# States in one software-queue load, a split first x load, and scores at other slots in an attention + GELU kernel

## Chip, cores, metric

One NeuronCore of a Trainium2 chip. The metric is the device time of one execution in microseconds (us), the median over several runs. The kernel before takes 268.34 us (three runs, 267.02 to 268.4). A profiled run adds a trace; its span, from first to last instruction, is some 2 us shorter than the device time. In the traces PE is TensorE (matmuls), PEld its weight loads, ACT is ScalarE (exp, GELU, copies), DVE is VectorE (copies, sums), POOL is GpSimd and SP is SyncE. A load issued by gpsimd goes through the software queue, one issued by SP or ACT through a hardware queue.

## The reference, cut to what matters

```python
# x: 8 batches x 8 heads x 512 x 64,  state: 8 x 8 x 32 x 64
scores = scale * x @ state.T            # softmax over 32 states   -> a
xread  = a @ state
scores2 = scale * state @ x.T           # softmax over 512 rows    -> a2
sread  = a2 @ x
h = concat([xread, sread], axis=2)      # -> 4352 rows x 512
out = gelu(h @ w_in) @ w_out            # w_in 512 x 2048, w_out 2048 x 512
```

The kernel folds `state @ w_in` into a matrix P per batch, so that `gelu(a @ P) @ w_out` gives the rows of xread.

## The kernel before

Names used below: `M` is one pair of matmuls into an `hp` PSUM buffer plus a GELU on ACT; `U` is four matmuls into an `op` buffer and, in its last quarter, a copy on DVE and a store from SP; `pmat` makes P. PSUM buffers are those that matmuls write; x^T is x transposed, A^T the transposed attention weights of xread. Batches 1 to 7 run in a loop of eight slot pairs `p`, two `M` each. Scores, `hp` and `p_ps` all share four PSUM buffers (`ps_f`).

The states of batches 1 to 7 come as fourteen loads from SP, after the first normalisation of batch 0. On the memory side the slowest dimension is `c`, four heads:

```python
st_rows = state.rearrange("b (c t) n d -> b t c n d", t=2)
...
def load_states():
    for b in range(1, B):
        for t in range(2):
            nc.sync.dma_start(out=st_f[:, b, t, :], in_=st_rows[b, t])
```

x of batch 0 comes in two software-queue (gpsimd) loads that cast to bf16. The order in the loop:

```python
for b in range(1, B):
    nb = b + 1
    for p in range(2 if b == 1 else 0, 8):
        k = 16 * b + 2 * p
        if p == 2 and nb < B:
            scores(nb, 0); scores(nb, 1); norm(nb, 0); norm(nb, 1)
        ...                       # p == 5: A^T of nb and x^T of nb + 1 by DMA transpose on SP
        M(k, k + 1)
        ...                       # last batch: also the rows of sread
        while u < k - 4:
            U(u); u += 1
        if p == (2 if b == 1 else 1):
            pmat(b, (2, 3), act=(1,))
            ...                   # and two U more, which leaves pair 2 without a U
```

The softmax here doesn't subtract the row's maximum and nothing guards it: scores larger than these inputs give would overflow.

Of the kernel before, what the change touches and what calls it, by code (L numbers as in the profile page):

```python
# [9 lines left out]
FP32 = mybir.dt.float32  # L10
BF16 = mybir.dt.bfloat16
# [6 lines left out]
def kernel(  # L18
# [8 lines left out]
    nc = tc.nc  # L27

    B, H, S, D = x.shape
    _, _, NS, _ = state.shape  # L30
# [3 lines left out]
    HC = H // 2  # L34
    MC = d_ff // 128
    SJ = S // 128
    FC = d_ff // 512

    persist = ctx.enter_context(tc.tile_pool(name="persist", bufs=1))
# [5 lines left out]
    ps_f = ctx.enter_context(tc.tile_pool(name="ps_f", bufs=4, space=PSUM))  # L45
# [8 lines left out]
    ident = persist.tile([128, 128], BF16, name="ident")  # L54
    sbd = persist.tile([128, B, HC, 2 * NS], BF16, name="sbd")
    XSR = persist.tile([128, HC, B * NS], BF16, name="XSR")
    g_sr = persist.tile([128, MC, B * NS], BF16, name="g_sr")
    st_f = persist.tile([128, B, 2, D], FP32, name="st_f")
    st_bf = persist.tile([128, B, 2, D], BF16, name="st_bf")
    gate = persist.tile([128, HC], FP32, name="gate")  # L60
    ones = persist.tile([128, HC], BF16, name="ones")
    warm = persist.tile([128, 512], BF16, name="warm")
    x4s = [persist.tile([128, SJ, HC, 128], BF16, name=f"x4_{i}") for i in range(2)]


    st_rows = state.rearrange("b (c t) n d -> b t c n d", t=2)
    for t in range(2):
        eng = nc.scalar if t == 0 else nc.sync
        eng.dma_start(out=st_f[:, 0, t, :], in_=st_rows[0, t])
    nc.vector.memset(warm, 0.0)  # L70
    nc.vector.memset(ones, 1.0)
    xbs = {0: xin.tile([128, H, SJ * D], BF16, name="xb", tag="xb")}
    xr = x.rearrange("b h (p j) d -> b p h (j d)", j=SJ)
    for i in range(2):
        hs = slice(4 * i, 4 * i + 4)
        nc.gpsimd.dma_start(out=xbs[0][:, hs, :], in_=xr[0, :, hs, :])
    make_identity(nc, ident)
    nc.vector.memset(sbd, 0.0)

    def load_w_in(f):  # L80
        nc.gpsimd.dma_start(
            out=w_in_bf[:, :, f * 512:(f + 1) * 512],
            in_=moe_w_in[:, f * 512:(f + 1) * 512].rearrange("(c p) f -> p c f", c=HC),
        )
# [6 lines left out]
    def load_x(b):  # L91
        xb = xin.tile([128, H, SJ * D], BF16, name="xb", tag="xb")
        nc.gpsimd.dma_start(out=xb, in_=xr[b])
        xbs[b] = xb
# [1 line left out]
    load_w_in(0)  # L96
    load_w_out(0)
    load_w_in(1)

    def load_states():  # L100
        for b in range(1, B):
            for t in range(2):
                nc.sync.dma_start(out=st_f[:, b, t, :], in_=st_rows[b, t])  # L103

    def load_rest():
        load_x(1)
# [8 lines left out]
    def keep_warm(n):  # L115
        ps = ps_o.tile([128, 512], FP32, name="warm_ps", tag="op")
        for _ in range(n):
            nc.tensor.matmul(ps, lhsT=warm[:, 0:128], rhs=warm, start=True, stop=True)


    def state_prep(b0, b1):
        n = b1 - b0
        nc.vector.tensor_copy(out=st_bf[:, b0:b1, :, :], in_=st_f[:, b0:b1, :, :])  # L123
        ps = ps_f.tile([128, n, HC, NS], BF16, name="st_ps", tag="f")
        for b in range(b0, b1):
            nc.tensor.transpose(  # L126
                ps[:, b - b0, :, :].rearrange("p c n -> p (c n)"),
                st_bf[:, b, :, :].rearrange("q t d -> q (t d)"),
                ident,
            )  # L130
        for t in range(2):
            src = ps[64 * t:64 * t + 64, :, :, :].rearrange("d b c n -> d (b c) n")
            dst = sbd[64 * t:64 * t + 64, b0:b1, :, 32 * t:32 * t + 32].rearrange(
                "d b c n -> d (b c) n"
            )
            nc.vector.tensor_copy(out=dst, in_=src)


    class Att:
# [2 lines left out]
    atts = {}  # L142

    def begin(b):
        A = Att()
        atts[b] = A
        A.x4 = x4s[b % 2]
        A.xT = att.tile([128, SJ, HC, 128], BF16, name="xT", tag="xT")
        A.e = att.tile([128, SJ * 2, HC * NS], BF16, name="e", tag="e")
        A.a = att.tile([128, SJ * 2, HC * NS], BF16, name="a", tag="a")  # L150

    def rearr(b):
        A = atts[b]
        eng = nc.vector if b < 2 else nc.gpsimd
        for t in range(2):
            eng.tensor_copy(  # L156
                out=A.x4[:, :, :, 64 * t:64 * t + 64].rearrange("p j c d -> p c j d"),
                in_=xbs[b].rearrange("p (c t) (j d) -> p t c j d", t=2, d=D)[:, t],
            )


    def xtr(b, cs):
        A = atts[b]
        xv = xbs[b].rearrange("p (c t) (j d) -> p j c t d", t=2, d=D)
        ps = ps_f.tile([128, len(cs), SJ, 128], BF16, name="xT_ps", tag="f")
        for i, c in enumerate(cs):
            for j in range(SJ):
                for t in range(2):
                    nc.tensor.transpose(ps[64 * t:64 * t + 64, i, j, :], xv[:, j, c, t, :], ident)  # L169
        out = A.xT[:, :, cs[0]:cs[0] + len(cs), :].rearrange("p j c n -> p c j n")  # L170
        if b == 0 and cs[0] == 0:
            nc.scalar.copy(out=out, in_=ps)
        else:
            nc.vector.tensor_copy(out=out, in_=ps)

    def xtr_dma(b):
        A = atts[b]
        nc.sync.dma_start_transpose(
            out=A.xT.rearrange("p j c n -> p (j c) n"),
            in_=A.x4.rearrange("p j c n -> p (j c n)"),  # L180
        )
# [68 lines left out]
    def atr(b):  # L250
        A = atts[b]
        A.AT = att.tile([128, SJ, 2, 128], BF16, name="AT", tag="AT")
        if b == 0:
            for t in range(2):
                ps = ps_f.tile([128, SJ, 128], BF16, name="aT_ps", tag="f")
                for j in range(SJ):
                    nc.tensor.transpose(ps[:, j, :], A.a[:, 2 * j + t, :], ident)
                o, i = A.AT[:, :, t, :], ps
                if t == 0:
                    nc.vector.tensor_copy(out=o, in_=i)  # L260
                else:
                    nc.scalar.copy(out=o, in_=i)
            return
        ps = ps_f.tile([128, 2, SJ, 128], BF16, name="aT_ps", tag="f")
        for t in range(2):
            for j in range(SJ):
                nc.tensor.transpose(ps[:, t, j, :], A.a[:, 2 * j + t, :], ident)
        nc.vector.tensor_copy(out=A.AT.rearrange("p j t n -> p t j n"), in_=ps)

    def atr_dma(b):  # L270
        A = atts[b]
        A.AT = att.tile([128, SJ, 2, 128], BF16, name="AT", tag="AT")
        nc.sync.dma_start_transpose(
            out=A.AT.rearrange("p j t n -> p (j t) n"), in_=A.a
        )
# [140 lines left out]
    def M(*ms):  # L416
        for m in ms:
            mm1(m // MC, m % MC)

    def U(*us):  # L420
        for u in us:
            mm2(u // 16, u % 16 // 4, u % 4)

    begin(0)
    keep_warm(6)
    state_prep(0, 1)
    xtr(0, (0, 1))
    scores0(0)
    scores0(1)
    xtr(0, (2, 3))  # L430
    norm0(0)
    nc.vector.memset(st_f[0:1, 1, 0, 0:1], 0.0)
    load_states()
    norm0(1)
    scores0(2)
    norm0(2)
# [5 lines left out]
    nc.scalar.activation(out=gate, in_=ones, func=AF.Gelu)  # L442
    keep_warm(3)
    atr(0)
    rearr(0)


    M(0, 1, 2, 3)
# [2 lines left out]
    U(2)  # L451
    M(4)
    U(3)
    state_prep(1, B)
    begin(1)
    xtr(1, (0, 1))
    xtr(1, (2, 3))
    M(5)
# [38 lines left out]
    u = 16  # L497
    for b in range(1, B):
        nb = b + 1
        for p in range(2 if b == 1 else 0, 8):  # L500
            k = 16 * b + 2 * p
            if p == 2 and nb < B:
                scores(nb, 0)
                scores(nb, 1)
                norm(nb, 0)
                norm(nb, 1)
            if p == 5 and nb < B:
                atr_dma(nb)
                if nb + 1 < B:
                    begin(nb + 1)  # L510
                    rearr(nb + 1)
                    xtr_dma(nb + 1)
                    if nb + 3 < B:
                        load_x(nb + 3)
            M(k, k + 1)
            if nb == B:
                mm1_sr(2 * p)
                mm1_sr(2 * p + 1)
            while u < k - 4:
                U(u)  # L520
                u += 1
            if p == (2 if b == 1 else 1):
                pmat(b, (2, 3), act=(1,))
            if p == 6 and nb < B:
                pmat(nb, (0, 1), act=(1,))
            if p == (2 if b == 1 else 1) or p == 6 and nb < B:
                if u >= 16:
                    U(u, u + 1)
                    u += 2
            if p == 4 and nb < B:  # L530
                sread(nb)
            if p == 6 and nb < B:
                srt(nb)
    while u < 16 * B - 4:
        U(u)
# [34 lines left out]
```

## Time and profile before

| | before |
|---|---|
| device time, median | 268.34 us |
| profiled span | 266.8 us |
| TensorE busy | 220.7 us (83%) |
| ACT, DVE busy | 121.3 us, 81.5 us |
| TensorE waits named by the trace | 24.3 (states), 5.7 (x^T of batch 2), 2.7 (exp), 2.4 (first x) us |

In the slices one digit is the busy share, in tenths, of one fortieth of the span; PEclk is the clock that the throttle granted to TensorE, in the same tenths. The wait view lists for each pair of instruction groups the total idle time, how often, and the longest. The lines themselves stand in the prediction.

### The profile page before, as it was taken

What the parts mean: (1) busy time and instruction counts of PE and PEld (TensorE: products, weight loads), DVE (VectorE), ACT (ScalarE), POOL (GpSimd) and SP (SyncE); (2) the same over time, 40 slices, a digit from 0 to 9 for tenths busy, and PEclk for the clock granted to TensorE, in tenths of its full rate; (3) what the DMA queues carried; (4) which work ended last, traced back from release to release, by engine and by line L of the source; (5) the groups of instructions that cost most, each with busy time, mean ns of one, the idle gap of its engine ahead of it and who ended that gap; (6) DMA issues with size and microseconds to landing.
All of it is one profiled execution on the core that took longest, in us unless ns stands there. A gap on an engine that the chain in (4) does not pass through costs nothing.

```text
span 266.8 us, 4389 instructions
## 1 busy us (share of the span) xinstructions
PE 220.7 (83%) x1867; PEld 101.8 (38%) x1867; DVE 81.5 (31%) x160; ACT 121.3 (45%) x214; POOL 28.7 (11%) x38
## 2 busy tenths in 40 slices
PE   4794000998918999999999989998998999999992
PEld 1431000643302444444444434444443445455540
DVE  2421000564516021912552172246025520500032
ACT  1371000282608344945574475449445745544200
POOL 6290000242000030040012003000000000000000
PEclk9999555699985899999999999999999999999999
DMA  7999992066260860466253047012903200400015
GB/s 89 192 172 186 202 144 40 2 79 80 79 157 1 120 79 3 157 123 76 81 133 66 0 157 109 11 77 83 122 0 143 56 4 0 158 2 0 0 41 195
DMA packets 38643, 22.82 MB, mean 86 GB/s; under 512 B 21856, under 2 KB 34400, under 8 KB 38624
## 3 DMA queue, kind: packets, MB, share of 16 engines
q0 software_dynamic: 12560, 8.39, 22.3%
q1 hardware_dynamic: 25788, 14.00, 21.2%
q8 instruction: 14, 0.23, 0.3%
q10 hardware_dynamic: 276, 0.16, 0.2%
q14 instruction: 5, 0.04, 0.0%
HBM read 17.30 MB, written 8.91 MB: 98 GB/s over the span
## 4 chain that ended last, share of the span: by engine, by line
PE 70%; SPq 9%; DMA 8%; ACT 5%; DVE 4%; issue 2%; DVEq 0%; ACTq 0%; POOLq 0%
PE op L376 38%; PE hp L346 18%; SPq L103 9%; DMA st_f<-in_state_dram 4%; PE p_ps L322 3%; PE hps L390 3%; PE ops L402 3%; DMA xb<-in_x_dram 2%; ACT L227 2%; DMA xT<-x 2%; PE sr L286 2%; PE xT_ps L169 1%; ACT e L227 1%; ACT g L353 1%; DVE a L243 1%
## 5 line engine op out<-in xcount | busy, mean ns | idle before, releaser
L376 PE MATMUL op<-w_out_bf,g 128*128 128x512 bf16 x512 | 123.8, 383 | 0.3
L353 ACT ACTIVATE g<-hp 128x512 bf16<-128x512 f32 x128 | 67.9, 601 | 84.5 <-PE hp L346 84.4
L376 PEld LDWEIGHTS <-g 128*128 128x128 bf16 x512 | 48.8, 98 | 63.2 <-issue 8.0
L346 PE MATMUL hp<-AT,P 128*128 128x512 bf16 x256 | 66.7, 388 | 3.1 <-ACT e L227 2.7
L346 PEld LDWEIGHTS <-P 128*128 128x128 bf16 x256 | 23.8, 99 | 31.0 <-issue 7.0
L336 DVE CAST P<-p_ps 128x512 bf16<-128x512 f32 x32 | 20.7, 684 | 39.2 <-PE p_ps L322 39.1
L366 DVE COPY osb<-op 128x512 f32<-128x512 f32 x31 | 20.8, 687 | 36.6 <-PE op L376 36.6
L334 ACT CAST P<-p_ps 128x512 bf16<-128x512 f32 x32 | 17.5, 588 | 24.0 <-PE p_ps L322 14.9
L156 POOL COPY x<-xb 128x1024 bf16<-128x1024 bf16 x12 | 12.6, 1083 | 129.7 <-PE sr L286 129.7
L126 PE MATMUL st_ps<-ident,st_bf 128*128 128x128 bf16 x8 | 1.2, 308 | 24.3 <-DVE st_bf L123 24.3
L227 ACT ACT_TABLE_LOAD x7 | 9.0, 1283 | 10.3 <-PE pt L220 6.7
L322 PE MATMUL p_ps<-w_in_bf,sbd 64*32 64x512 bf16 x256 | 12.4, 403 | 1.3 <-ACT g L353 1.3
L240 DVE TENSOR_REDUCE cs<-e 128x16 f32<-128x512 bf16 x14 | 9.5, 681 | 12.9 <-ACT e L227 12.9
L243 DVE TENSOR_TENSOR a<-e,ics 128x512 bf16<-128x512 bf16 x14 | 10.5, 750 | 0.6
L126 PEld LDWEIGHTS <-st_bf 128*128 128x128 bf16 x8 | 0.8, 136 | 25.6 <-DVE st_bf L123 25.6
L220 PE MATMUL pt<-sbd,xT 128*128 128x64 bf16 x112 | 4.8, 200 | 5.7 <-DMA xT<-x 5.7
L366 DVE COPY osb<-ops 128x512 f32<-128x512 f32 x2 | 1.4, 692 | 26.3 <-PE ops L402 26.3
L353 ACT ACT_TABLE_LOAD x7 | 9.0, 1283 | 0.1
L123 DVE CAST st_bf<-st_f 128x128 bf16<-128x128 f32 (+1 forms) x2 | 0.9, 426 | 26.5 <-DMA st_f<-in_state_dram 26.5
L390 PE MATMUL hps<-XSR,w_in_bf 128*128 128x256 bf16 x64 | 8.3, 273 | 0.0
L295 DVE RECIPROCAL inv<-sr 128x2 f32<-128x2 f32 x8 | 1.4, 169 | 21.9 <-PE sr L286 21.9
L227 ACT ACTIVATE e<-pt 128x512 bf16<-128x512 f32 x14 | 7.6, 594 | 0.1
(55 smaller groups left out, 104.6 us busy)
## 6 DMA issues: line engine op xcount, KB each, us to landing
out_dram<-osb SPq DMA_DIRECT2D x31, 256.0 KB
xb<-in_x_dram POOLq DMA_DIRECT2D x7, 512.0 KB, 6.8
w_in_bf<-in_moe_w_in_dram POOLq DMA_DIRECT2D x4, 512.0 KB, 11.6
w_out_bf<-in_moe_w_out_dram POOLq DMA_DIRECT2D x4, 512.0 KB, 12.2
xb<-in_x_dram POOLq DMA_DIRECT2D x2, 256.0 KB, 5.4
out_dram<-osb SPq DMA_DIRECT2D x8, 64.0 KB
st_f<-in_state_dram SPq DMA_DIRECT2D x15, 32.0 KB
out_dram<-osb SPq DMA_DIRECT2D x1, 128.0 KB
```

What stands on the lines that cost most here:

```text
L103: nc.sync.dma_start(out=st_f[:, b, t, :], in_=st_rows[b, t])
L156: eng.tensor_copy(out=A.x4[:, :, :, 64 * t:64 * t + 64].rearrange("p j c d -> p c j d"), in_=xbs[b].rearrange("p (c t) (j d) -> p t c j d" ...
L227: nc.scalar.activation(out=A.e[:, :, 64 * half:64 * half + 64], in_=pt.rearrange("p j t c n -> p (j t) (c n)"), func=AF.Exp, scale=scale,)
L243: nc.vector.tensor_tensor(out=A.a[:, :, hs].rearrange("p g (c n) -> p g c n", n=NS), in0=e4, in1=ics[:, :, :].to_broadcast((128, G, 2, NS) ...
L322: nc.tensor.matmul(ps[t][32 * c:32 * c + 32, :], lhsT=sbd[64 * t:64 * t + 64, b, c, 32 * t:32 * t + 32], rhs=w_in_bf[64 * t:64 * t + 64, c ...
L334: nc.scalar.copy(out=dst, in_=ps[t])
L336: nc.vector.tensor_copy(out=dst, in_=ps[t])
L346: nc.tensor.matmul(hp, lhsT=Ps[b][:, t, m * 128:(m + 1) * 128], rhs=atts[b].AT[:, :, t, :], start=(t == 0), stop=(t == 1),)
L353: nc.scalar.activation(out=gs[b][:, m, :], in_=hp, func=AF.Gelu)
L366: nc.vector.tensor_copy(out=osb, in_=ps)
L376: nc.tensor.matmul(ps, lhsT=gs[b][:, m, j * 128:(j + 1) * 128], rhs=w_out_bf[:, m, :], start=(m == 0), stop=(m == MC - 1),)
L390: nc.tensor.matmul(hp, lhsT=w_in_bf[:, c, m * 128:(m + 1) * 128], rhs=XSR[:, c, :], start=(c == 0), stop=(c == HC - 1),)
```

## The change

It means to take away each of the four waits: states as one bf16 load on the software queue, early; x of batch 0 half over the hardware queue as fp32 and half over the software queue, so that both halves come sooner, with x^T copied in quarters; and the next batch's scores at another slot pair. Core of the diff:

```diff
-    st_rows = state.rearrange("b (c t) n d -> b t c n d", t=2)
+    st_rows = state.rearrange("b (e h) n d -> (h n) b e d", e=2)
+    nc.scalar.dma_start(out=st_f, in_=st_rows[:, 0, :, :])
+    for c in range(2):
+        nc.sync.dma_start(out=x0f[:, 2 * c:2 * c + 2, :], in_=xr[0, :, 2 * c:2 * c + 2, :])
...
+    nc.gpsimd.dma_start(out=xbs[0][:, 4:8, :], in_=xr[0, :, 4:8, :])
...
     load_w_in(1)
-    def load_states(): ...            # fourteen nc.sync.dma_start
+    nc.gpsimd.dma_start(
+        out=st_bf[:, 1:B, :, :].rearrange("q b e d -> q (b e) d"),
+        in_=st_rows[:, 1:B, :, :].rearrange("q b e d -> q (b e) d"),
+    )
...                                    # state_prep: four half transposes a batch; x^T in quarters;
...                                    # A^T in two halves, both copied on DVE
-            if p == 2 and nb < B:
+            if p == (4 if b == 1 else 1) and nb < B:
                 scores(nb, 0)
...
-            if p == 5 and nb < B:
+            if p == (7 if b == 1 else 4) and nb < B:
                 atr_dma(nb)
-                if nb + 1 < B:
+            if p == (7 if b == 1 else 5) and nb + 1 < B:
...
-            if p == (2 if b == 1 else 1):
+            if p == 3:
                 pmat(b, (2, 3), act=(1,))
...
-            if p == 4 and nb < B:
+            if p == 5 and nb < B:
                 sread(nb)
```

More of the change, by code (lines that the diff above doesn't have):

```diff
@@ L57 @@
     g_sr = persist.tile([128, MC, B * NS], BF16, name="g_sr")
-    st_f = persist.tile([128, B, 2, D], FP32, name="st_f")
+    st_f = persist.tile([128, 2, D], FP32, name="st_f")
     st_bf = persist.tile([128, B, 2, D], BF16, name="st_bf")
+    x0f = persist.tile([128, HC, SJ * D], FP32, name="x0f")
     gate = persist.tile([128, HC], FP32, name="gate")
@@ L63 @@
     x4s = [persist.tile([128, SJ, HC, 128], BF16, name=f"x4_{i}") for i in range(2)]
-    st_rows = state.rearrange("b (c t) n d -> b t c n d", t=2)
-    for t in range(2):
-        eng = nc.scalar if t == 0 else nc.sync
-        eng.dma_start(out=st_f[:, 0, t, :], in_=st_rows[0, t])
+    xr = x.rearrange("b h (p j) d -> b p h (j d)", j=SJ)
+    st_rows = state.rearrange("b (e h) n d -> (h n) b e d", e=2)
+    nc.scalar.dma_start(out=st_f, in_=st_rows[:, 0, :, :])
+    for c in range(2):
+        nc.sync.dma_start(out=x0f[:, 2 * c:2 * c + 2, :], in_=xr[0, :, 2 * c:2 * c + 2, :])
     nc.vector.memset(warm, 0.0)
@@ L72 @@
     xbs = {0: xin.tile([128, H, SJ * D], BF16, name="xb", tag="xb")}
-    xr = x.rearrange("b h (p j) d -> b p h (j d)", j=SJ)
-    for i in range(2):
-        hs = slice(4 * i, 4 * i + 4)
-        nc.gpsimd.dma_start(out=xbs[0][:, hs, :], in_=xr[0, :, hs, :])
+    nc.gpsimd.dma_start(out=xbs[0][:, 4:8, :], in_=xr[0, :, 4:8, :])
     make_identity(nc, ident)
@@ L98 @@
     load_w_in(1)
-    def load_states():
-        for b in range(1, B):
-            for t in range(2):
-                nc.sync.dma_start(out=st_f[:, b, t, :], in_=st_rows[b, t])
+    nc.gpsimd.dma_start(
+        out=st_bf[:, 1:B, :, :].rearrange("q b e d -> q (b e) d"),
+        in_=st_rows[:, 1:B, :, :].rearrange("q b e d -> q (b e) d"),
+    )
     def load_rest():
@@ L121, in state_prep @@
     def state_prep(b0, b1):
+        if b0 == 0:
+            nc.scalar.copy(out=st_bf[:, 0, :, :], in_=st_f)
         n = b1 - b0
-        nc.vector.tensor_copy(out=st_bf[:, b0:b1, :, :], in_=st_f[:, b0:b1, :, :])
-        ps = ps_f.tile([128, n, HC, NS], BF16, name="st_ps", tag="f")
+        ps = ps_f.tile([128, n, 2, 2, 2, NS], BF16, name="st_ps", tag="f")
         for b in range(b0, b1):
-            nc.tensor.transpose(
-                ps[:, b - b0, :, :].rearrange("p c n -> p (c n)"),
-                st_bf[:, b, :, :].rearrange("q t d -> q (t d)"),
-                ident,
-            )
-        for t in range(2):
-            src = ps[64 * t:64 * t + 64, :, :, :].rearrange("d b c n -> d (b c) n")
-            dst = sbd[64 * t:64 * t + 64, b0:b1, :, 32 * t:32 * t + 32].rearrange(
-                "d b c n -> d (b c) n"
-            )
-            nc.vector.tensor_copy(out=dst, in_=src)
+            for e in range(2):
+                for t in range(2):
+                    nc.tensor.transpose(
+                        ps[64 * t:64 * t + 64, b - b0, e, :, :, :].rearrange("d u t n -> d (u t n)"),
+                        st_bf[:, b, e, :],
+                        ident,
+                    )
+        for t in range(2):
+            nc.vector.tensor_copy(
+                out=sbd[64 * t:64 * t + 64, b0:b1, :, 32 * t:32 * t + 32].rearrange(
+                    "d b c n -> d (b c) n"
+                ),
+                in_=ps[64 * t:64 * t + 64, :, :, :, t, :].rearrange("d b e u n -> d (b e u) n"),
+            )
     class Att:
@@ L159, in rearr, with cast0, rearr0 @@
             )
+    def cast0(c):
+        nc.vector.tensor_copy(
+            out=atts[0].x4[:, :, c, :].rearrange("p j (t d) -> p t j d", t=2),
+            in_=x0f[:, 2 * c:2 * c + 2, :].rearrange("p t (j d) -> p t j d", d=D),
+        )
+    def rearr0():
+        A = atts[0]
+        for t in range(2):
+            nc.vector.tensor_copy(
+                out=A.x4[:, :, 2:4, 64 * t:64 * t + 64].rearrange("p j c d -> p c j d"),
+                in_=xbs[0].rearrange("p (c t) (j d) -> p t c j d", t=2, d=D)[:, t, 2:4],
+            )
     def xtr(b, cs):
@@ L167, in xtr @@
             for j in range(SJ):
+                if b == 0 and c < 2:
+                    nc.tensor.transpose(ps[:, i, j, :], A.x4[:, j, c, :], ident)
+                    continue
                 for t in range(2):
@@ L170, in xtr @@
         out = A.xT[:, :, cs[0]:cs[0] + len(cs), :].rearrange("p j c n -> p c j n")
-        if b == 0 and cs[0] == 0:
+        if b == 0 and cs[0] % 2 == 0:
             nc.scalar.copy(out=out, in_=ps)
@@ L252, in atr @@
         A.AT = att.tile([128, SJ, 2, 128], BF16, name="AT", tag="AT")
-        if b == 0:
-            for t in range(2):
-                ps = ps_f.tile([128, SJ, 128], BF16, name="aT_ps", tag="f")
-                for j in range(SJ):
-                    nc.tensor.transpose(ps[:, j, :], A.a[:, 2 * j + t, :], ident)
-                o, i = A.AT[:, :, t, :], ps
-                if t == 0:
-                    nc.vector.tensor_copy(out=o, in_=i)
-                else:
-                    nc.scalar.copy(out=o, in_=i)
-            return
-        ps = ps_f.tile([128, 2, SJ, 128], BF16, name="aT_ps", tag="f")
         for t in range(2):
+            ps = ps_f.tile([128, SJ, 128], BF16, name="aT_ps", tag="f")
             for j in range(SJ):
-                nc.tensor.transpose(ps[:, t, j, :], A.a[:, 2 * j + t, :], ident)
-        nc.vector.tensor_copy(out=A.AT.rearrange("p j t n -> p t j n"), in_=ps)
+                nc.tensor.transpose(ps[:, j, :], A.a[:, 2 * j + t, :], ident)
+            nc.vector.tensor_copy(out=A.AT[:, :, t, :], in_=ps)
     def atr_dma(b):
@@ L425 @@
     keep_warm(6)
+    cast0(0)
+    cast0(1)
     state_prep(0, 1)
-    xtr(0, (0, 1))
+    xtr(0, (0,))
+    xtr(0, (1,))
     scores0(0)
     scores0(1)
-    xtr(0, (2, 3))
+    xtr(0, (2,))
+    xtr(0, (3,))
     norm0(0)
-    nc.vector.memset(st_f[0:1, 1, 0, 0:1], 0.0)
-    load_states()
     norm0(1)
@@ L444 @@
     atr(0)
-    rearr(0)
+    rearr0()
     M(0, 1, 2, 3)
@@ L453 @@
     U(3)
-    state_prep(1, B)
+    state_prep(1, 4)
+    state_prep(4, B)
     begin(1)
@@ L506 @@
                 norm(nb, 1)
-            if p == 5 and nb < B:
+            if p == (7 if b == 1 else 4) and nb < B:
                 atr_dma(nb)
-                if nb + 1 < B:
-                    begin(nb + 1)
-                    rearr(nb + 1)
-                    xtr_dma(nb + 1)
-                    if nb + 3 < B:
-                        load_x(nb + 3)
+            if p == (7 if b == 1 else 5) and nb + 1 < B:
+                begin(nb + 1)
+                rearr(nb + 1)
+                xtr_dma(nb + 1)
+                if nb + 3 < B:
+                    load_x(nb + 3)
             M(k, k + 1)
@@ L525 @@
                 pmat(nb, (0, 1), act=(1,))
-            if p == (2 if b == 1 else 1) or p == 6 and nb < B:
-                if u >= 16:
-                    U(u, u + 1)
-                    u += 2
-            if p == 4 and nb < B:
+            if p == 3 or p == 6 and nb < B:
+                U(u, u + 1)
+                u += 2
+            if p == 5 and nb < B:
                 sread(nb)
-            if p == 6 and nb < B:
+            if p == 7 and nb < B:
                 srt(nb)
```

## The prediction

> **What bounds the kernel now.** I read the page's slices first, then the waits of TensorE, the windows, the chain that ended last, and the landings of single DMAs. The slices:
>
> ```profile
> PE   4794000998918999999999989998998999999992
> PEclk9999555699985899999999999999999999999999
> DMA  7999992066260860466253047012903200400015
> ```
>
> One digit is 6.67 us. TensorE is full nearly everywhere except in slices 4 to 6 (zero), 11 and 12, and its granted clock drops in those holes and stays low behind them. So the bound is TensorE, plus holes. Its waits name them (total, times, longest):
>
> ```profile
> PE st_ps L126 <- DVE st_bf L123: 24.3, 1, 24.3
> PE pt L220 <- DMA xT<-x: 5.7, 1, 5.7
> PE hp L346 <- ACT e L227: 2.7, 3, 0.9
> PE xT_ps L169 <- DMA xb<-in_x_dram: 2.4, 1, 2.4
> ```
>
> Four waits, and the change aims at all four. The timeline and the chain of waits tell what stands behind the first:
>
> ```profile
> 11.62 26.43 SPq L103 DMA_DIRECT2D st_f<-in_state_dram  x14
> ...
> 35.91 10.57 DMA st_f<-in_state_dram
> 46.60 0.64 DVE st_bf L123
> ```
>
> The 14 state loads are handed to the SP queue at 11.6 us, take 26.4 us merely to issue behind the weights, and the last lands at 46.6. TensorE has nothing from 22.98 to 47.28. The windows (length, busy time of each engine, PEclk, DMA share, GB/s) give what a hole costs afterwards:
>
> ```profile
> 23.00:46.60 23.60, 0.00 (x0) 0.00 (x0) 0.00 (x1) 0.00 (x0) 0.00 (x0) 0.59 0.91 139
> 74.00:79.50 5.50, 0.07 (x2) 0.08 (x3) 0.42 (x1) 0.00 (x0) 0.00 (x0) 0.91 0.69 159
> 79.50:89.00 9.50, 8.21 (x45) 2.98 (x46) 4.37 (x8) 5.80 (x8) 0.00 (x0) 0.51 0.39 44
> 89.00:109.00 20.00, 20.00 (x182) 8.81 (x180) 4.76 (x10) 10.13 (x19) 2.84 (x3) 1.00 0.38 71
> ```
>
> The 5.7 us wait for the transposed x of batch 2 is followed by 9.4 us at half clock. The undisturbed pace is in the timeline at the first scores of batches 3 to 5:
>
> ```profile
> 109.10 0.63 PE L220 MATMUL pt<-sbd,xT 128*128 128x64 bf16 x16
> ...
> 132.40 0.63 PE L220 MATMUL pt<-sbd,xT 128*128 128x64 bf16 x16
> ...
> 155.70 0.63 PE L220 MATMUL pt<-sbd,xT 128*128 128x64 bf16 x16
> ```
>
> One batch takes 23.30 us of pure TensorE work. From batch 2's scores (79.42) to batch 3's (109.10) it took 29.7 us: 6.4 lost to the clock. The next two periods (scores at 155.70, 180.14, 204.54) are 24.4, so each holds 1.1 us of waiting.
>
> **What the Trainium skill says.** (1) "TensorE: Matmul & The Clock Gate", Part 1: an idle window of about 3.4 us drops the array to half clock, and about as much busy time restores it. The trace agrees on the halving (clock 0.51; eight 512-column matmuls take 3.37 us instead of 1.73), but the return took some 9 us, not 3.4, probably because this stage is itself broken by short waits. (2) "DMA: Bandwidth & Descriptors", "Why a DMA increments its semaphore by 16 and not by 1": a DMA spreads over the largest k up to 16 that divides the slowest dimension of both its sides. The old state load has 4 on the memory side (four heads), hence 4 engines; the new one has 128 rows, hence 16. The trace fits: from 40 to 44 us the DMA share is 0.34 at 46 GB/s, a few engines draining late, while 180 to 200 GB/s is usual. (3) Same page, "Specifications": transfers under 512 B miss line rate and are read-modify-written. The new state load writes 128 B rows; nothing in this trace has that form on the software queue. (4) "ScalarE: Activation LUTs", "What ACT_TABLE_LOAD costs": 1283 ns, and a drain of 1380 ns. The trace has 1283 ns and no visible drain (exp starts 0.02 us after the load).
>
> **The change, part by part.**
>
> *States by one software DMA.* It stands behind w_in(0), w_out(0), w_in(1) and before x(1). Landings, from start of issue plus time to landing: w_in(1) 4.90 + 10.9 = 15.8; x(1) 13.44 + 7.3 = 20.7; w_out(1) 24.1, w_in(2) 27.3, w_out(2) 30.7, w_in(3) 34.0, w_out(3) 37.5. Those after x(1) come 3.3 us apart, the first three weights only 2.6: I put the difference down to the four engines that also carry state packets, since a DMA ends with its slowest engine. The new load has 7 x 2 x 128 = 1792 packets, 112 per engine. From 4 to 6 us the queue did 704 packets of 512 B (16 x 2 / 704 = 45 ns each per engine), from 8 to 10 us 390 of 1 KB (82 ns); the line through both gives 17 ns at 128 B. Allowing up to 45 ns for the small-write penalty, 1.9 to 5 us. x(0) now comes half on another queue, so the weights start about 1.1 us earlier: states land at 15.8 - 1.1 + 1.9 to 5 = 16.6 to 19.7, x(1) 2.7 later at 19.3 to 22.4. TensorE reaches the state transposes at about 20.5 (below) and x(1) at about 22. The 24.3 us wait should go whole: **-24.3**. The weights then land at 2.7 us steps, w_out(1) at 22 to 25 and w_in(2) at 25 to 28. They are wanted 5.8 and 7.6 us after the state transposes start (53.06 and 54.88 against 47.28), so at about 26.5 and 28.5, later ones with more slack. More work: 28 half transposes at 0.066 us (16 take 1.07) instead of 7 at 0.133: **+0.8**. Matmuls that ran cold at 47 to 51 us run warm: **-0.4**.
>
> *Prologue.* Before, x landed at 6.45 and 7.7 (issue 1.24, to landing 5.2), the transposes started at 6.50, DVE copied at 10.32 to 11.01, then four times sum and reciprocal and one multiply (2.85 us) to 13.89, and the matmuls of M(0) ran without pause from 16.26. The state load issued at 0.74 by the hardware queues was used at 3.57. With 256 KB pieces I guess 4.2 and 5.3 for the two x pieces and 6.6 for the software half. Working through the queue of each engine: casts (0.43 each, from 0.626 for 896 columns) end at 4.65 and 5.75, state copies 6.25, quarter copies of 0.43 (DVE) or 0.57 (ACT), the last at about 8.5 instead of 11.0; the same 2.85 us chain ends at 11.4. Both AT copies on DVE (2 x 0.43) replace one that waited on ACT's table load. That is 2.5 to 3.2 us; w_in(0), landing at 9.4, may hold part back. I take **-2.5**.
>
> *Scores later in batch 1 (fourth slot pair index instead of second).* In front of the wait now lie 4 M (1.73), 4 U (3.46) and a pmat (0.56) = 5.75 us, against 5.74 us of waiting: **-5.7**, with **+0.5** for what may stay over. No idle window then, so no half clock: **-6.4**. But in that slot two M pairs follow the scores without a U between, and with four PSUM buffers the second pair waits for exp and its table load: **+1.0** once.
>
> *Scores in the second pair of later slots.* The 1.1 us waits of three batches come from the same crowding: four pmat buffers before, scores, then M, M with no U (the pair's U had been pulled forward). Now a U pair (1.73 us) stands between, and pmat has moved to pair 3: exp frees its buffers at 2.35 us after the scores at worst, M wants them at 3.07. **-3.3**. The output copies on DVE now queue behind the 3.9 us normalisation; they end 6.4 us after the scores at worst, the bank is wanted at 6.5. **0**.
>
> Sum: 266.8 - 24.3 + 0.8 - 0.4 - 2.5 - 5.7 + 0.5 - 6.4 + 1.0 - 3.3 = 226.5 us of span. The profiled run took 268.62 for its 266.8, so 1.8 more: **228 us**.
>
> **Rivals.** (a) *The state load takes the place of the wait*: at 100 ns per small packet it would last 11 us, states would land at 26 and x(1) at 28.5; TensorE would wait some 6 us and run cold behind it, about 238 to 240. For: the form is unseen, and it stands before x(1). Against: the queue kept 45 ns at 512 B. (b) *DMA supply becomes the bound of the first 45 us*: if the weights keep their 3.3 us steps and shift by the state load, w_in(2) lands at about 29 to 30, and small waits of 1 to 2 us sum up: 231 to 233. For: the queue runs at 180 to 200 GB/s without pause. Against: every later weight has more slack. (c) *The half-clock stage stays*: x^T still goes out behind four output stores on SP, and if it lands more than 3 us after TensorE gets there, the clock falls again: 234 to 238. Against: it must be 3 us later than before relative to the work. (d) *The new order is worse in steady state*, DVE's late output copies holding U by 0.5 to 1 us in five batches: 231 to 233. For: the margin is only 0.1 us.
>
> **Range and chances.** The three large terms (24.3, 5.7, 6.4) are independent of any guess on durations if nothing else arrives late; a and c each have about one chance in ten, b and d together one in four. Everything better than planned reaches 222. I say 222 to 236. To be within 2% of the old time nearly everything would have to be given back.
>
> **What would show it.** Right: TensorE's wait for the states under 1 us, slices 3 to 7 full, PEclk 9 from start to end, 23.3 us between scores of all batches, first M matmul at 13 to 14 us, no table-load wait in later batches. Wrong: a wait at the state transposes or x(1) (rival a), at w_out or w_in (b), a PEclk of 5 around 45 to 55 us (c), waits of U on the output copy (d).

## The result

The changed kernel takes **228.56 us** (median of four, 228.31 to 229.13) against 268.13 us of the kernel before in the same rounds. The ratio is 0.8534, with a 95% interval of 0.8504 to 0.8564. Ratios here are the mean time of one kernel's runs over that of the other's of the same rounds, so they are not quite the ratio of the medians quoted. Executions over 1.5% slower than the fastest of the same kernel are left out of the means. The predicted 228 us was hit; the terms behind it were not all hit, as shown below. The profiled span is 226.5 us.

The slices of the changed kernel (one digit is now 5.66 us):

```profile
PE   7699999977999999999999999999999999999991
PEclk9799999996999999999999999999999999999999
DMA  6999997991590917075009400750061002200025
```

The hole of three zeros is gone. Besides the opening, one shallow dip is left in slices 8 and 9 (counted from 0, as in the prediction), with a PEclk of 6 in slice 9. TensorE's waits in the changed kernel:

```profile
PE pt L241 <- DMA xT<-x: 2.8, 1, 2.8
PE warm_ps L116 <- DVE ones L73: 1.2, 1, 1.2
PE pc L209 <- ACT xT L193: 0.7, 2, 0.5
PE xT_ps L190 <- DMA xb<-in_x_dram: 0.6, 1, 0.6
```

No wait for the states and none for exp; the wait for x^T of batch 2 is halved, not gone. The landing of the state load (from the DMA view) and the timeline of the state transposes:

```profile
st_bf<-in_state_dram POOLq DMA_DIRECT2D x1, 224.0 KB, 11.7
```

```profile
4.89 1.11 POOL L98 DMA_DIRECT2D st_bf<-in_state_dram  x1
...
19.33 0.97 PE L128 MATMUL st_ps<-ident,st_bf 128*64 128x128 bf16 x28
```

Issued at 4.89, landed at 16.6, used at 19.33: 2.7 us to spare. The third load of the weights before it (issue 4.16, to landing 10.9) landed at 15.1, so the 1792 small packets took 1.5 us. The transpose of x of batch 2, in the chain of waits before, then after:

```profile
74.88 4.50 DMA xT<-x
```

```profile
44.86 7.43 DMA xT<-x
```

The remaining dip in the windows (start:end, length, busy times of PE, weight loads, DVE, ACT, POOL, PEclk, DMA share, GB/s):

```profile
44.90:49.50 4.60, 4.60 (x35) 1.62 (x32) 1.29 (x2) 2.36 (x5) 0.00 (x0) 1.00 1.27 271
49.50:52.30 2.80, 0.00 (x0) 0.00 (x0) 0.00 (x0) 0.00 (x0) 0.00 (x0) 1.00 0.91 181
52.30:56.40 4.10, 3.94 (x25) 1.68 (x26) 1.43 (x3) 3.46 (x4) 0.00 (x0) 0.58 0.02 4
```

The transpose was issued at 44.86 and landed 7.43 us later; before it took 4.50. The matmuls put in front of it lasted to 49.50, so 2.8 us stayed open, and then came 3.4 us at half clock (52.79 to 56.20 by PEclk in windows of 0.1 us; over the longer window shown it averages 0.58). The half clock alone did not cost time that the runs show: one of the four was granted 1.00 on average and took 228.73 us, two were granted 0.985 and took 228.31 and 228.38. Later all is even:

```profile
67.41 0.64 PE L241 MATMUL pt<-sbd,xT 128*128 128x64 bf16 x16
...
90.72 0.63 PE L241 MATMUL pt<-sbd,xT 128*128 128x64 bf16 x16
```

23.31 us, and the later periods are the same (114.03, 137.34, 160.60). Split at two points that both traces have, the 40.3 us of span go like this:

| stretch | before | after | difference | predicted |
|---|---|---|---|---|
| start to the state transposes of batches 1 to 7 | 47.28 | 19.33 | -27.95 | -26.8 |
| to the last output copy of batch 0 (73.72, 43.69) | 26.44 | 24.36 | -2.1 | +0.4 |
| to the end | 193.1 | 182.8 | -10.3 | -13.9 |

### The profile page after: what moved, and what is told of

It reads as the page before. It is cut to its first block, busy times and chain, and to the rows that moved or that the text cites. A ratio compares the mean times of both kernels' runs of the same rounds, so it can differ in the third digit from the quotient of the medians.

```text
span 226.5 us, 4400 instructions
## 1 busy us (share of the span) xinstructions
PE 214.7 (95%) x1883; PEld 99.0 (44%) x1883; DVE 81.2 (36%) x164; ACT 121.2 (54%) x215; POOL 28.5 (13%) x38
## 4 chain that ended last, share of the span: by engine, by line
PE 83%; DMA 7%; DVE 3%; ACT 3%; issue 1%; SPq 1%; POOL 1%; DVEq 0%; POOLq 0%; ACTq 0%
PE op L386 45%; PE hp L356 22%; PE p_ps L332 4%; DMA xT<-x 3%; DMA w_in_bf<-in_moe_w_in_dram 3%; PE hps L400 3%; PE ops L412 3%; PE sr L296 2%; ACT g L363 2%; PE pt L241 1%; DMA out_dram<-osb 1%; SPq L378 1%; DVE osb L376 1%; PE warm_ps L116 1%; DVE a L264 1%
## 5 line engine op out<-in xcount | busy, mean ns | idle before, releaser
L386 PE MATMUL op<-w_out_bf,g 128*128 128x512 bf16 x512 | 122.4, 379 | 0.3
L376 DVE COPY osb<-op 128x512 f32<-128x512 f32 x31 | 20.0, 685 | 12.2 <-PE op L386 12.2
L159 POOL COPY x<-xb 128x1024 bf16<-128x1024 bf16 x12 | 12.1, 1043 | 97.0 <-PE sr L296 58.2
L248 ACT ACT_TABLE_LOAD x7 | 9.0, 1283 | 5.7 <-PE pt L241 4.3
L332 PE MATMUL p_ps<-w_in_bf,sbd 64*32 64x512 bf16 x256 | 10.8, 389 | 0.4 <-DMA w_in_bf<-in_moe_w_in_dram 0.4
L264 DVE TENSOR_TENSOR a<-e,ics 128x512 bf16<-128x512 bf16 x14 | 9.7, 692 | 0.6
L363 ACT ACT_TABLE_LOAD x7 | 9.0, 1283 | 0.1
L400 PEld LDWEIGHTS <-w_in_bf 128*128 128x128 bf16 x64 | 6.3, 98 | 2.4
L412 PE MATMUL ops<-w_out_bf,g_sr 128*128 128x512 bf16 x32 | 7.1, 379 | 0.0
```

Source lines behind the costliest of these rows:

```text
L159: eng.tensor_copy(out=A.x4[:, :, :, 64 * t:64 * t + 64].rearrange("p j c d -> p c j d"), in_=xbs[b].rearrange("p (c t) (j d) -> p t c j d" ...
L248: nc.scalar.activation(out=A.e[:, :, 64 * half:64 * half + 64], in_=pt.rearrange("p j t c n -> p (j t) (c n)"), func=AF.Exp, scale=scale,)
L264: nc.vector.tensor_tensor(out=A.a[:, :, hs].rearrange("p g (c n) -> p g c n", n=NS), in0=e4, in1=ics[:, :, :].to_broadcast((128, G, 2, NS) ...
L332: nc.tensor.matmul(ps[t][32 * c:32 * c + 32, :], lhsT=sbd[64 * t:64 * t + 64, b, c, 32 * t:32 * t + 32], rhs=w_in_bf[64 * t:64 * t + 64, c ...
L363: nc.scalar.activation(out=gs[b][:, m, :], in_=hp, func=AF.Gelu)
L376: nc.vector.tensor_copy(out=osb, in_=ps)
```

## The experiments

The theory: the old state loads were late because of their shape (few engines a load, many issues), not because of their queue; the parts of the change lean on one another; the wait that is left comes from an x load that runs beside the transpose; and the exp waits came from PSUM buffers crowded by two `M` pairs in a row. Eleven runs, all correct. Times are medians.

| run | time, us | ratio to before |
|---|---|---|
| states part alone | 241.80 | 0.904 |
| slot order alone | 256.17 | 0.955 |
| changed, first x again by software queue | 231.46 | 0.865 |
| changed, states by one SP load | 230.00 | 0.858 |
| changed, states by fourteen SP loads of 128 rows | 234.50 (three fast runs) | 0.877 |
| changed, x^T of batch 2 ahead of the stores | 226.85 | 0.847 |
| changed, x of batches 4 and 5 loaded early | 226.47 | 0.846 |
| changed, scores in pair 4 of all batches | 233.96 | 0.873 |
| x early and x^T of batch 3 early | 225.12 | 0.840 |
| the same, scores of batch 2 in pair 5 | 231.78 | 0.865 |
| changed, again | 228.88 | 0.854 |

### States alone, order alone

The kernel before with only the state hunks:

```diff
-    load_states()                       # fourteen SP loads
+    nc.gpsimd.dma_start(out=st_bf[:, 1:B]..., in_=st_rows[:, 1:B]...)
+    # state_prep of the changed kernel; x and slots as before
```

> The kernel before with only the state loads changed (one software DMA behind w_in(1), state transposes as in the change). Theory: the wait of 24.3 us goes whole, and the stage behind it is about 2 us shorter (no half clock, less collision on DVE), but the wait for x^T of batch 2 grows from 5.7 to some 8.5 us, because the last x load is now still in flight when the transpose runs (as in the changed kernel, where it took 7.4 us instead of 4.5): about 244 us. Rival, the parts add up without touching each other: 268.1 - 24.3 - 2.2 = 241.6 with the x^T wait still at 5.7.

Measured: 241.80 us (241.24 to 244.08). TensorE's longest wait in its trace:

```profile
PE pt L221 <- DMA xT<-x: 6.6, 1, 6.6
```

The state wait went whole. The wait for x^T grew from 5.7 to 6.6, not to 8.5: here the transpose was issued at 46.93 and took 5.3 us. The time alone speaks for the rival (parts that simply add up), the trace for an effect of the theory's kind at a third of the size. I count this as a half miss.

The kernel before with only the loop of the changed kernel:

```diff
-            if p == 2 and nb < B:
+            if p == (4 if b == 1 else 1) and nb < B:
     # and the other conditions of the loop as in the changed kernel
```

> The kernel before with only the order inside the slots changed. Theory: here the x loads have long landed when x^T of batch 2 is transposed (4.5 us), so the 5.75 us of matmuls put in front cover it whole: wait under 0.3 us, no half clock, the three waits for exp of 0.9 us gone, about 1 us of exp wait once; 268.1 - 5.7 - 6.4 - 3.3 + 1 = about 254 us. Rival, the order alone gives what it gave in the changed kernel (10.1 us behind the end of batch 0): 258 us, with a wait of about 2.8 us left.

Measured: 256.17 us (255.37 to 256.38), between the two. Its waits:

```profile
PE st_ps L126 <- DVE st_bf L123: 26.3, 2, 25.9
...
PE hp L346 <- ACT e L227: 1.0, 1, 1.0
...
PE pt L220 <- DMA xT<-x: 0.6, 1, 0.6
```

The mechanism is the theory's: no wait at the scores of batch 2, no half clock behind them, one exp wait of 1.0. The 0.6 is at batch 3, whose transpose took 7.7 us, with an x load issued 0.35 us after it. From the last output copy of batch 0 (74.44) to the end of the span (254.5) it takes 180.1 us, against 193.1 before (266.8 - 73.7): 13.0 less, where the prediction had 13.9 and the changed kernel shows 10.3. So the slot order is worth its predicted sum as long as no load runs beside the transpose of batch 2. Besides, the unbroken run of `M` matmuls started 1.3 us sooner in this run (14.94 us instead of 16.26), yet the state transposes began at 47.46 instead of 47.28: while the states bound the kernel, an earlier start was worth nothing.

### The first x load

```diff
-    nc.sync.dma_start(out=x0f[...], in_=xr[0, ...])      # fp32, two pieces
+    for i in range(2):
+        nc.gpsimd.dma_start(out=xbs[0][:, 4*i:4*i+4, :], in_=xr[0, :, 4*i:4*i+4, :])
```

> The changed kernel with x of batch 0 again by two software DMAs (transposed in half tiles, no fp32 copy), quarters and all else kept. Theory: of the 3.6 us by which M(0) starts earlier, most is the hardware-queue load: x lands at 6.45 instead of 3.8 and w_in(0) at 10.5 instead of 9.9, so +1.5 to +2.5 us: 230 to 231 us. Rival, the quarter copies and the AT copies on DVE are the gain: within 0.5 us of the changed kernel.

Measured: 231.46 us (230.96 to 232.53), 2.9 us slower, a little over the range. Only part of it is the start: the state transposes began at 20.59 instead of 19.33 (1.26 us). The rest lies 30 us later: the x^T wait of batch 2 is 4.2 instead of 2.8 us, for its transpose (issued 46.11) took 8.8 us. Its software load landed at 5.3 us, as in the two runs above (5.2 and 5.3), while the profiled run of the kernel before had it at 6.45. So about 1.2 us of the "3.6 us of prologue" that the two first profiles show is one slow first load in one trace.

Taken together, the times add up: 25.5 us for the states alone, 11.2 for the order alone and these 2.9 make 39.6, and the whole change gained 268.13 - 228.56 = 39.6. That the parts lean on one another shows in the waits for x^T (5.7, 6.6, 2.8 us), not in the sum.

### What made the old state loads late

```diff
-    nc.gpsimd.dma_start(out=st_bf[:, 1:B]..., in_=st_rows[:, 1:B]...)
+    nc.sync.dma_start(out=st_f[:, 1:B]..., in_=st_rows[:, 1:B]...)   # fp32, after norm0(0); cast on DVE
```

> The changed kernel with the states of batches 1 to 7 by one fp32 DMA on the SP queue at 11.5 us, where the kernel before issued its fourteen, but with 128 rows on the slow side, and the cast on DVE. Theory: what made them late was the spread over 4 engines and the fourteen issues, not the queue: they land before 20 us and the time is within 1 us of the changed kernel. Rival, small packets on the hardware queue starve behind the weights on the software queue: they land after 30 us, TensorE waits over 10 us and the time is above 240 us.

Measured: 230.00 us (228.82 to 231.26), 1.4 us above the changed kernel where at most 1 was expected. The states landed at 19.88, and TensorE waited twice for the DVE cast, 2.7 us together. The hardware queue is not the cause. Two things differ from the old loads, though: one issue instead of fourteen, and 128 rows instead of four on the slow side. To part them:

```diff
+    for b in range(1, B):
+        for e in range(2):
+            nc.sync.dma_start(out=st_f[:, b, e, :], in_=st_rows[:, b, e, :])   # 128 rows each
```

> The changed kernel with the states on the SP queue in fourteen DMAs again, but each with 128 rows on the slow side of both access patterns[...]. This parts the two things that the run with one SP load changed together. Theory A, the spread over 4 engines held the old loads up: states land at about 20 us as with one SP load, time within 1.5 us of it (230 us). Theory B, the fourteen issues held them up (each issue waits for room behind the weights): the last issue ends after 25 us, TensorE waits over 6 us, over 236 us.

Measured: 234.50 us (233.75 to 236.89; a fourth run, slow, is left out). The issues of the state load on SP, first with fourteen 128-row loads, then with one:

```profile
9.32 9.20 SPq L101 DMA_DIRECT2D st_f<-in_state_dram  x14
```

```profile
8.95 0.37 SPq L99 DMA_DIRECT2D st_f<-in_state_dram  x1
```

| states | issuing takes | last landing |
|---|---|---|
| fourteen, four heads outermost (before) | 26.4 us | 46.6 us |
| fourteen, 128 rows outermost | 9.2 us | 26.0 us |
| one, 128 rows outermost | 0.4 us | 19.9 us |
| one on the software queue (changed) | 1.1 us | 16.6 us |

Neither theory holds alone. With the number of loads the same, the shape accounts for 20.6 us of landing (some 2 us of it because issuing began 2.3 us earlier); the number for 6.1 us more. TensorE waited 5.7 us in the fourteen-load run and ran at a clock of 0.62 from 26.5 to 32.0. That the shape acts through the number of DMA engines is the rule of the Trainium skill that the prediction takes from "DMA: Bandwidth & Descriptors" ("Why a DMA increments its semaphore by 16 and not by 1"), and it fits the low DMA share late in the kernel before; but no run here counts engines, and the new shape also makes each load one stretch of 32 KB in memory instead of four of 8 KB. The two are not parted.

### What is left of the x^T wait

Two edits, one theory each. First, hand the transpose to SP before the output stores:

```diff
+    begin(2); rearr(2); xtr_dma(2); load_x(4)
     U(12)
     M(16, 17)
     ...
-    begin(2); rearr(2); xtr_dma(2); load_x(4)      # stood behind U(15)
```

> The changed kernel with x^T of batch 2 handed to SP before the four output stores of batch 0 instead of behind them (x of batch 2 is rearranged at 37.4 us, so it can go at about 38). It then has over 10 us before the scores of batch 2. Theory: the 2.8 us wait and the half clock behind it (window 52.3 to 56.4, where 8 M matmuls take 3.7 us instead of 1.9) go: 228.6 - 2.8 - 2 = about 224 us, granted clock 1.00 at 50 to 60 us. Rival, the stage is bound elsewhere (by the exp of batch 2 or by the later transpose of batch 3): under 1 us is gained.

Measured: 226.85 us (225.34 to 228.36). In the trace the wait for x^T of batch 2 is gone and the clock is 1.00 from 44 to 70 us, but only 1.7 us were gained, not 4.6. The six runs fall into two groups, 225.3 to 225.8 and 227.9 to 228.4 us; the trace is of the first, and what the others did is not known. Second, leave SP alone and take the x loads out of the way:

```diff
-    xin = ctx.enter_context(tc.tile_pool(name="xin", bufs=3))
+    xin = ctx.enter_context(tc.tile_pool(name="xin", bufs=6))
...
         load_x(3)
+        load_x(4)
+        load_x(5)                        # and not again later
```

> The changed kernel with six x buffers and x of batches 4 and 5 loaded right behind x of batch 3, so that no load runs when x^T of batch 2 is transposed; the order on SP is untouched. Theory: the transpose took 7.4 us instead of 4.5 because the load of batch 5 (issued 40.5, landed 50.2) ran beside it; now it takes 4.5 us or less, TensorE waits under 0.5 us and the time is about 224 us. Rival, the four output stores in front of it are what holds it: it still takes about 7 us and the time stays at 228 to 229 us.

Measured: 226.47 us (226.42 to 227.12). The timeline of SP and of TensorE's scores:

```profile
45.35 2.01 SPq L201 DMA_TRANSPOSE xT<-x  x1
...
49.87 0.64 PE L243 MATMUL pt<-sbd,xT 128*128 128x64 bf16 x16
```

With the same four stores ahead of it, the transpose took 4.5 us again, by the DMA view, and TensorE did not wait. So a load beside it was the cause, not the stores: that of batch 5, which ran from 40.53 to 50.2 in the changed kernel (batch 4's had landed at 43.8, before the transpose was issued). The rival is refuted. Other traces agree for x^T of batch 2: 5.3 and 5.4 us where a load landed 1 to 2 us after the issue (states alone, one SP load), 4.5 where none ran (fourteen SP loads), 8.2 beside two loads (the run above). Not every overlap hurts, though: with x again by the software queue, x^T of batch 3 took 4.5 us although a load was issued 1.07 us after it, while one issued 0.94 us after it in the changed kernel went with 7.8. Why is open. The gain is 2.1 us instead of 4.6. Of the missing 2.5, 1.0 is a wait for exp, which the dip had hidden, and 0.9 one at the scores of batch 3 (none in the first profile of the changed kernel, 0.8 in its repeat below), whose transpose meets the load of batch 6:

```profile
PE hp L358 <- ACT e L250: 1.0, 1, 1.0
PE pt L243 <- DMA xT<-x: 0.9, 1, 0.9
```

So I gave that transpose an earlier place too:

```diff
-            if p == (7 if b == 1 else 5) and nb + 1 < B:
+            if p == (3 if b == 1 else 5) and nb + 1 < B:
                 begin(nb + 1); rearr(nb + 1); xtr_dma(nb + 1)
```

> The kernel with the six x buffers, and in addition x^T of batch 3 handed to SP in slot pair 3 of batch 1 instead of pair 7 (x of batch 3 is rearranged at 40.5 us). Theory: the 0.9 us wait at the scores of batch 3 (its transpose ran beside the load of batch 6) goes, and nothing else changes: 225.5 us. Rival, the wait moves to the next thing (A^T of batch 2 behind it in the queue): no gain over 226.5 us.

Measured: 225.12 us (224.35 to 225.97), beside 228.88 of the unaltered changed kernel in the same rounds, a ratio of means of 225.14 / 228.84 = 0.984. It beats both kernels. The 0.9 us wait is gone; the 1.0 us for exp stays. The unaltered kernel, for comparison:

> The changed kernel unaltered, beside the others on the same chip: 228.5 us as before. It shows what differs from run to run in the first 13 us and in the wait for x^T of batch 2 (2.8 us in the first profile).

It again waited 3.0 us for x^T of batch 2, and 0.8 us at batch 3, so the dip is not a chance of the first profile.

### Crowded PSUM buffers

```diff
-            if p == (4 if b == 1 else 1) and nb < B:
+            if p == 4 and nb < B:            # A^T and x^T of all batches at pair 7
```

> The changed kernel with the next batch's scores in slot pair 4 of all batches (right behind pmat's four buffers, M pairs without U following), not in pair 1. Theory: crowding of the four PSUM buffers makes the waits for exp, so a wait of about 0.9 us comes in each of five batches: about +4 us, 232 to 233 us. Rival, the waits of the kernel before came from where the table load stands on ACT and not from the missing U: no more than +1 us.

Measured: 233.96 us (233.56 to 234.87), somewhat over the expected range, with these waits:

```profile
PE hp L356 <- ACT e L248: 4.7, 5, 1.0
PE pt L241 <- DMA xT<-x: 3.3, 1, 3.3
...
PE hp L356 <- DMA AT<-a: 1.0, 1, 1.0
```

Five exp waits of up to 1.0 us are back, as the theory has it. The rival is half right all the same: there are six batches with scores in the loop and five waits. At batch 3 ACT had its table loaded ahead of the scores (77.44 against 78.14) and no wait came, just as at batches 3 and 4 of the kernel before. In the changed kernel the load starts late once (at 91.19, after the scores began at 90.72) without a wait; there a `U` pair follows. So in these traces it takes both: a late table load and no `U` behind the `M` pair. Why the load is late in some batches is open. The last miss:

```diff
-            if p == (4 if b == 1 else 1) and nb < B:
+            if p == (5 if b == 1 else 1) and nb < B:
```

> The kernel of the run before in this call, and the scores of batch 2 in slot pair 5, where a U pair follows, instead of pair 4. Theory (crowding of PSUM buffers): the one exp wait of 1.0 us goes, 224.5 us. Rival: A^T of batch 2 is then too late for the first M of batch 2 and a wait of 1 to 2 us takes its place, 225 to 226.5 us.

Measured: 231.78 us (230.34 to 233.0), 6.7 us worse than without the edit. The exp wait went; the rival came, larger than it said:

```profile
PE hp L358 <- DMA AT<-a: 5.1, 1, 5.1
```

A^T of batch 2, issued at 57.02 just behind the load of batch 6 (56.20), took 8.9 us to land; in the run before and in the changed kernel it takes 3.1 and 3.3. It is the same collision, with another transpose.

## Why the prediction was right

The total, 228 against 228.56 us, is right because the largest terms were read from waits that really ended, and because three misses cancelled: the predicted span of 226.5 us is to the digit the measured one, and that is luck.

- **States, -24.3.** Right, with its mechanism. The landing of 16.6 is the early end of the predicted 16.6 to 19.7: the small packets took 1.5 us, 13 ns each and engine, where I allowed 17 to 45. Rivals (a) and (b) failed: after it the weights landed 2.6 us apart, 22.3 for w_out(1) and 24.9 for w_in(2), as the 2.7 us steps had it.
- **Prologue, -2.5.** It came to -3.65 between the two traces. Some 1.2 us of that is the slow first load in the trace of before. The undo run gives 1.26 us to the hardware-queue x load; what the quarter copies and the DVE copies of A^T did singly was not run. The `M` matmuls began at 12.67, before the 13 to 14 us named as a sign.
- **State transposes, +0.8, and warm matmuls, -0.4.** Wrong sign in sum: this stretch is 2.1 us shorter. 28 half transposes took 0.97 us in all, not 28 x 0.066 (whose sum, less 7 x 0.133, is +0.9, not +0.8). I had taken that duration from a row of the opening, where matmuls still ran at half pace (six warm-up matmuls in 2.74 us) although the windows print a PEclk of 1.00 there. The 32 transposes of x(1) took 1.06 instead of 1.92, and the wait of 1.08 us for the transpose of `srm` shrank to 0.3; there a multiply on DVE that took 1.51 us beside a POOL copy now takes 0.69. That the POOL copy caused it is argued, not tested.
- **x^T wait, -5.7 + 0.5, and no half clock, -6.4.** The step that failed: I took the 4.5 us of the transpose as fixed. Once the states no longer held TensorE, the transpose moved 30 us forward (issue 74.88 to 44.86) but the load of batch 5 only 20 (60.74 to 40.53), and the two met; the transpose took 7.4 us. It left 2.8 us instead of 0.5, and the clock fell for 3.4 us. The early-load run shows the cause. Rival (c) thus came true in a small form, at less than the 3 us that it named. The 6.4 us were also misread as "lost to the clock": in the kernel before TensorE ran at half clock from 79.42, when it had work again, to 88.72, which can cost at most 4.7 us, and it stood idle for 1.3 us of that time, waiting for a GELU. The order-only run, 13.0 us of 13.9, shows that taking off the whole was right all the same. The half-clock window of the Trainium skill is free-running ("TensorE: Matmul & The Clock Gate", Part 1), which fits that waits of 2.8 and 3.0 us lowered the clock here, while one of 3.3 us in the pair-4 run did not (PEclk 1.00 from 52.3 to 67.4).
- **Exp once, +1.0.** Right, but hidden: in the changed kernel it lies inside the half-clock stage, whose stretch between the scores of batches 2 and 3 takes 15.1 us; with x^T early it takes 15.4 including 1.0 and 0.9 of waits, so 13.5 bare. The dip's clock and the exp wait thus cost 1.5 together, where 1.0 was planned. Of the 3.6 us missing in the last row of the table, 2.3 are the x^T wait and 0.5 this; 0.8 stay unplaced.
- **Exp waits of batches 5 to 7, -3.3.** Right in size: every later period is 23.3 us, and crowding brings the waits back. As a cause crowding is half of it: the kernel before had the same order at batches 3 and 4, and no wait, with the table loaded early. Rival (d), late output copies, did not come: the table of waits has none.

## What to carry to other kernels

When the largest wait goes, what was merely early before becomes late: re-place every transfer whose slack came from that wait, above all loads that may run beside a DMA transpose something waits for. A load's access pattern is part of its cost: the same bytes on the same queue landed at 46.6 or at 26.0 us by the dimension that stands outermost (2 us of it from an earlier issue), and at 19.9 us as one DMA. And check each term of a prediction that came out right; here three of them were off by 1 to 4 us.

## What the Trainium skill lacked or had wrong

- "DMA: Bandwidth & Descriptors" gives a transpose's bandwidth but not what a load beside it costs: in the changed kernel and its variants x^T mostly took 4.3 to 4.5 us without one (5.3 to 5.5 for batch 6 in most of these runs, unexplained), and 7.4 to 8.8 us where a 512 KB software-queue load ran beside most of it, with the exception told above; A^T mostly took 3.1 to 3.4 us (5.0 to 5.2 for batch 5, unexplained), and 8.9 us just behind one (scores of batch 2 in pair 5).
- The same page ("Issuing engines are not separate DMA queues") calls the time to initiate a DMA usually small: fourteen 32 KB loads took SP 26.4 us to issue with four heads outermost, and 9.2 us with 128 rows.
- The same page ("Specifications") names read-modify-write for transfers under 512 B; the page prices small descriptors, but not this: 1792 packets that write 128 B added 1.5 us to the queue here, 13 ns each and engine, about in proportion to the 45 ns at 512 B in the kernel before (11 ns), so no penalty shows.
- "TensorE: Matmul & The Clock Gate" has about 3.4 us for both ways of the half clock. For the fall that is no safe limit: waits of 2.8 and 3.0 us sufficed here, one of 3.3 us did not. For the return the traces agree: the half clock lasted 3.4 us in the changed kernel (52.79 to 56.20) and 10.2, three times that, in the kernel before (78.48 to 88.72), where TensorE was busy for only 2.5 and 2.1 us of the first two thirds and for all of the last.
- "ScalarE: Activation LUTs" adds a drain of 1380 ns to each table load: in these traces exp mostly starts 0.01 to 0.02 us after the 1283 ns load (54.19 to 54.20 in the changed kernel), the load can start 0.02 us after the operation before it (108.40 in the kernel before), and no drain is seen.
